# Attention with a linear branch: one step of VectorE's exponentials moved to GpSimd, with batches of four tiles

## The chip, the cores and the metric

One core of a Trainium2 chip. The metric is device time in microseconds, from runs of the whole kernel; a profile of one execution shows its span from the first to the last instruction. Engines in the text: TensorE (PE) multiplies matrices into PSUM, ScalarE (ACT) computes the exponentials, VectorE (DVE) and GpSimd (POOL) do elementwise work, SyncE (SP) issues DMAs.

## The reference

Two attention branches over the same 2048 tokens of width 512 (32 heads of 16) are mixed by a gate:

```python
g = sigmoid((x * gate_w).sum(-1, keepdims=True))
# branch A: plain softmax attention
scores = einsum("bhqd,bhkd->bhqk", q, k) * (Dh ** -0.5)
a = (softmax(scores) @ v, heads merged) @ wo
# branch B: linear attention with softmax features
phi_q = concat([softmax(q @ w_phi), softmax(-(q @ w_phi))])      # phi_k likewise
b = (phi_q @ (phi_k^T v) / (phi_q @ sum(phi_k) + 1e-6)) @ wo
return g * a + (1 - g) * b
```

Branch A's scores are 32 x 2048 x 2048 numbers, and each needs an exponential. That is the bulk of the work.

## The kernel before

**Tiles.** A score tile is 128 keys by 512 queries of one head, keys on partitions. The run goes through 512 packs (`NPACK`) of four tiles (four heads), in 32 groups of 16 packs: a group is one query chunk with four heads, and its 16 packs run over the keys. `_scores` (L977, matmuls L984) makes a tile in a PSUM bank; `_exp` (L1027, L1035) lets ScalarE take groups of three and two tiles alternately to `ET`; `_pv` (L1042, matmuls L1104) multiplies each tile by the values into the accumulator of its group; `_norm` divides and transposes on VectorE (L1157 to L1169). Five of the eight banks are the ring for ScalarE, three are shared by accumulators, projections and VectorE's tiles. The last group is cut into four blocks of 128 queries, so that its results come out one after the other.

**VectorE's tiles.** ScalarE can't do all exponentials in the time, so some tiles are done by VectorE. `SHARES` (L824) says how many in each of the 32 groups (226 in all), `SOON` adds four at the start; `_plan_vector` (L831) spreads them and cuts them into batches of `NB` = 5. `_vector_batch` (L862) makes 2^y of a batch by a cubic:

1. `v_bits` (L883), once a tile: the score from PSUM, scaled, as a uint32 fixed-point number into `vt` (two buffers, used in turn).
2. `v_frac` (L907): byte 2 of each word, the fraction, becomes an fp16 number in `vf` (one buffer).
3. `v_line` (L909), `v_sq` (L910), `v_cube` (L911): the polynomial, in `vf` and `vu` (three buffers, `NVU`).
4. `v_out` (L893): the integer part of `vt` is added to the result's bits, which then are a bf16 number.

Steps 2 to 4 work on a whole batch. The value matmuls of these tiles read `vu`.

**Branch B.** `_b_keys` and `_b_queries` project tokens and run `_b_part` (L1255), a long list of VectorE instructions (L1306 to L1359) that makes the feature softmaxes in bf16 and fp16; it uses `vt` and `vf` as scratch too. Its due times come from `K0, SK, Q0, SQ` (L1172).

**Order.** Nothing is scheduled at run time. `Plan.op` (L93) records every operation with its engine, a cost in microseconds, its buffers and a due time `prio`. `Plan.order` (L153) then walks through time with these costs: for each engine it takes the operations whose inputs are there and appends the one that can start first, the more urgent of two. The result is one fixed queue for each engine; `_waits` (L326) adds the semaphores that the dependencies need, and `emit` writes it out. An engine runs its queue strictly in order, so that an instruction that waits holds all that stand behind it. `LEAD` = 13 packs is how far ahead of its use a batch of VectorE is due. GpSimd has only constants to make, all near the start.

## Time and profile before

| what | us |
|---|---|
| median of 3 runs | 838.36 (837.57 to 838.61) |
| span of the profiled execution | 836.5 |
| VectorE's bits, L883, 226 of 512 columns | 148.3 |
| VectorE's `v_frac`, L907, 47 instructions | 67.1 |
| VectorE's `v_line` L909, `v_sq` L910, `v_cube` L911 | 37.9, 68.6, 68.5 |
| VectorE's `v_out`, L893 | 127.6 |

A line of the page's groups reads: line, engine and operation, output and input by the program's names, their shape and type, the count; then busy time and the mean length of one in ns; then the idle time of the engine in front of them and what ended it. A line of the stretches gives, for each engine, busy time and the number of instructions, then TensorE's granted clock (1.00 throughout), the DMA engines' busy share and GB/s. The time between the span and the runs' time lies outside the first and last instruction.

### The profile page before, as it was taken

The page shows a single profiled execution, that of the slowest core. Times are in us where ns is not written, and L with a number is a line of the kernel's source. Part 1 is how long each engine was busy: PE and PEld are TensorE (multiplying, and loading weights), DVE is VectorE, ACT ScalarE, POOL GpSimd, SP SyncE. Part 2 cuts the span into 40 slices and gives each one's busy share as a digit, 9 for nine tenths or more (in the row PEclk, how much of TensorE's full clock was granted, in tenths as well). Part 3 has the DMA queues.
Part 4 walks back from the last instruction along what each step waited for, and adds up shares of the span by engine and source line. Part 5 has one row for each costly group of instructions (what it writes and reads, how often), then busy time and mean ns, then how long its engine had stood idle before and what let it go on. Part 6 is the DMA issues. An engine that isn't in the chain of part 4 may idle for free.

```text
span 836.5 us, 19540 instructions
## 1 busy us (share of the span) xinstructions
PE 792.9 (95%) x8711; PEld 263.0 (31%) x8753; DVE 806.8 (96%) x1050; ACT 825.4 (99%) x733; POOL 8.0 (1%) x15
## 2 busy tenths in 40 slices
PE   9999999999999999999999999999999999999998
PEld 4323333333232222232223322222322223222234
DVE  6999999999999999999999999999998999999994
ACT  7999999999999999999999999999999999999997
POOL 3000000000000000000000000000000000000000
PEclk9999999999999999999999999999999999999999
DMA  9500000000000000210003010003100003000000
GB/s 250 157 6 8 1 7 1 2 1 8 2 7 2 7 1 8 52 22 13 1 7 59 20 33 2 4 5 70 27 15 8 1 11 79 21 8 2 2 2 27
DMA packets 49027, 20.01 MB, mean 24 GB/s; under 512 B 38704, under 2 KB 48944, under 8 KB 48944
## 3 DMA queue, kind: packets, MB, share of 16 engines
q1 hardware_dynamic: 48272, 18.58, 9.4%
q8 instruction: 68, 1.11, 0.6%
q10 hardware_dynamic: 672, 0.20, 0.1%
q14 instruction: 15, 0.12, 0.0%
HBM read 6.31 MB, written 2.10 MB: 10 GB/s over the span
## 4 chain that ended last, share of the span: by engine, by line
ACT 92%; DVE 5%; PE 2%; DMA 0%; SPq 0%; issue 0%
ACT ET L1035 92%; DVE vt L883 1%; PE ps L984 0%; DMA qT<-qraw 0%; SPq L761 0%; PE ps L633 0%; DVE vu L893 0%; PE ps L1113 0%; DVE bq L1268 0%; DVE vt L1321 0%; DVE VB L1252 0%; DVE T L1157 0%; DVE vf L907 0%; DVE vu L911 0%; DVE vf L910 0%; DVE bq L1315 0%
## 5 line engine op out<-in xcount | busy, mean ns | idle before, releaser
L1035 ACT ACTIVATE ET<-ps 128x1536 bf16<-128x1536 f32 x728 | 823.1, 1397 | 1.7 <-PE ps L984 1.5
L984 PE MATMUL ps<-qT,kT 32*128 32x512 bf16 (+2 forms) x2249 | 318.4, 364 | 31.4 <-ACT ET L1035 22.2
L1113 PE MATMUL ps<-kT,zero 128*32 128x512 bf16 (+1 forms) x3052 | 255.3, 383 | 0.0
L1104 PE MATMUL ps<-ET,V 128*32 128x512 bf16 (+2 forms) x1998 | 195.8, 364 | 1.3 <-ACT ET L1035 0.6
L984 PEld LDWEIGHTS ps<-qT,kT 32*128 32x128 bf16 x2249 | 83.5, 91 | 305.5 <-ACT ET L1035 227.1
L883 DVE TENSOR_SCALAR vt<-ps 128x512 uint32<-128x512 f32 x226 | 148.3, 681 | 3.8 <-PE ps L984 3.1
L893 DVE SCALAR_TENSOR_TENSOR vu<-vt,vu 128x2560 int16<-128x2560 uint32 (+3 forms) x47 | 127.6, 2716 | 0.7
L1113 PEld LDWEIGHTS ps<-kT,zero 128*32 128x32 bf16 x3052 | 67.9, 94 | 103.2 <-issue 78.5
L1104 PE MATMUL ps<-vu,V 128*32 128x512 bf16 (+1 forms) x250 | 85.3, 364 | 0.3 <-DVE vu L893 0.3
L1104 PEld LDWEIGHTS ps<-ET,V 128*32 128x32 bf16 x1998 | 55.0, 95 | 67.0 <-issue 36.9
L910 DVE TENSOR_TENSOR vf<-vf 128x2560 f16<-128x2560 f16 (+3 forms) x49 | 68.6, 1400 | 0.6
L911 DVE TENSOR_TENSOR vu<-vu,vf 128x2560 f16<-128x2560 f16 (+3 forms) x49 | 68.5, 1398 | 0.5
L907 DVE TENSOR_SCALAR vf<-vt 128x2560 f16<-128x2560 uint8 (+3 forms) x47 | 67.1, 1427 | 0.2
L681 PE MATMUL ps<-WB,xT 128*128 128x512 bf16 x165 | 48.8, 383 | 4.0 <-issue 1.6
L909 DVE TENSOR_SCALAR vu<-vf 128x2560 f16<-128x2560 f16 (+3 forms) x49 | 37.9, 774 | 2.0 <-PE ps L1104 1.8
L681 PE MATMUL ps<-xT,WA 128*128 128x512 bf16 (+1 forms) x124 | 35.8, 380 | 0.0
L1157 DVE STREAM_TRANSPOSE T<-ps 128x512 f32<-128x512 f32 (+1 forms) x35 | 23.2, 664 | 5.0 <-PE ps L1104 4.6
L1104 PEld LDWEIGHTS ps<-vu,V 128*32 128x32 bf16 x250 | 22.9, 96 | 11.5 <-issue 8.5
L681 PEld LDWEIGHTS ps<-WB,xT 128*128 128x128 bf16 x192 | 14.4, 97 | 27.0 <-issue 14.3
L1268 DVE TENSOR_SCALAR bq<-ps 128x512 bf16<-128x512 f32 x32 | 21.5, 679 | 0.5 <-PE ps L681 0.4
L777 PE MATMUL ps<-WA,xT 128*128 128x128 bf16 x256 | 18.9, 220 | 0.4 <-DVE vt L883 0.2
L1321 DVE TENSOR_TENSOR vt<-vt,brec 128x4096 bf16<-128x4096 bf16 (+1 forms) x10 | 18.6, 1857 | 0.0
(105 smaller groups left out, 421.8 us busy)
## 6 DMA issues: line engine op xcount, KB each, us to landing
qT<-qraw SPq DMA_DIRECT2D x120, 16.0 KB, 1.8
xn<-in_A_x_dram SPq DMA_DIRECT2D x3, 512.0 KB, 6.1
WB<-in_B_wqkv_dram SPq DMA_DIRECT2D x3, 512.0 KB, 5.0
out_dram<-WB SPq DMA_DIRECT2D x12, 128.0 KB, 1.9
WA<-in_A_wqkv_dram SPq DMA_DIRECT2D x3, 384.0 KB, 5.2
xn<-in_A_x_dram SPq DMA_DIRECT2D x2, 256.0 KB, 3.6
WoA<-in_A_wo_dram SPq DMA_DIRECT2D x1, 512.0 KB, 5.7
WoB<-in_B_wo_dram SPq DMA_DIRECT2D x1, 512.0 KB, 6.6
```

The costliest lines, as they stand in the source:

```text
L681: mm = op("PE", lambda e, c=c: e.matmul(self._bank(job)[:, 0:n], lhs(c), rhs(c), start=(c == 0), stop=(c == 3)), self.c_pe(n), reads=reads ...
L883: parts.append(op("DVE", lambda e, j=j, job=job: e.tensor_scalar(vt[:, j, :], self._bank(job), SCALE * LOG2E * 2.0 ** 24, 2.0 ** 31, op0=A ...
L893: o = op("DVE", lambda e: e.scalar_tensor_tensor(out=flat(vu).bitcast(I16), in0=flat(vt), scalar=2.0 ** -17, in1=flat(vu), op0=ALU.mult, o ...
L907: ("_frac", two, lambda e: e.tensor_scalar(vf, frac, 1 / 256, ROOT, op0=ALU.mult, op1=ALU.add), [b_vt], [b_vf]),
L909: lambda e: e.tensor_scalar(vu, vf, CUBE, SQUARE, op0=ALU.mult, op1=ALU.add), [b_vf], [b_vu]),
L910: ("_sq", two, lambda e: e.tensor_tensor(vf, vf, vf, ALU.mult), [b_vf], [b_vf]),
L911: ("_cube", two, lambda e: e.tensor_tensor(vu, vu, vf, ALU.mult), [b_vf, b_vu], [b_vu]),
L984: ins = e.matmul(out[u][:, cols], self.kT[32 * i:32 * i + 32, cp, kt * TOK:(kt + 1) * TOK], self.qT[32 * i:32 * i + 32, s, q], start=True, ...
L1035: o = plan.op("ACT", lambda e: e.activation(self.ET[:, a % NS:a % NS + n, :], self.ps[:, a % NR:a % NR + n, :], ACT.Exp, scale=SCALE), sel ...
L1104: ins = e.matmul(self._bank(ot)[32 * i:32 * i + 32, to], self.V[:, kt, g8 // 2, v0:v0 + 32], tile[:, cols], start=first and j == 0, stop=o ...
L1113: ins = e.matmul(self._bank(ot)[32 * i:32 * i + 32, lo:QCH], self.zero[:], self.kT[:, 0, lo:QCH], start=False, stop=False, tile_position=( ...
L1157: return e.transpose(to, acc if alone else acc.rearrange("p (e b d) -> p e b d", e=2, b=8))
```

## The change

The `v_frac` step of VectorE's tiles goes to GpSimd. A batch is four tiles, and GpSimd gets it in pieces of two, each of which waits only for the bits of its own two tiles, for the last readers of `vf`, and for the `v_out` of the batch before. The two small batches of `SOON` and the last two batches (`TAIL`) keep the step on VectorE. [...] `vt` has three buffers; a batch's score matmuls wait for the `v_cube` of the batch that used its buffer before, and its bits for all of that batch's readers. The shares are new (231 tiles and the four of `SOON`), as are several due times.

```diff
+        self.port = name in Plan.PORT
...
+    PORT = {"v_frac", "v_line", "v_sq", "v_cube", "v_out", "gate_z", "gate_h", "gate_b", "n_den", "n_mul", "kvbd", "b_grid", "b_rest",
+            "b_max", "b_top", "b_down", "b_square", "b_slope", "b_even", "b_odd", "b_part", "b_out", "b_sum", "b_ratio", "b_mul"}
+    GUARD, GIVE, TAKE = 0.25, 0.15, 0.12
...
+        port = {"DVE": None, "POOL": None}
...
+            pool = [(max(free["POOL"], o.dep_t, port["DVE"].end + self.GIVE if port["DVE"] else 0.0), o) for o in avail["POOL"]
+                    if o.port and o.rel <= self.now]
+            booked = min(pool, key=lambda x: x[0]) if pool else None
...
                     t = max(free[e], o.dep_t)
+                    if o.port and e == "POOL" and port["DVE"]:
+                        t = max(t, port["DVE"].end + self.GIVE)
+                    elif o.port and e == "DVE":
+                        if port["POOL"]:
+                            t = max(t, port["POOL"].end + self.TAKE)
+                        if booked and t > booked[0] - self.GUARD:
+                            t = max(t, booked[0] + booked[1].cost + self.TAKE)
...
+            if o.port and e in port:
+                other = port["DVE" if e == "POOL" else "POOL"]
+                if other is not None:
+                    o.deps.append(other)
+                port[e] = o
...
-    NB, NVU, LEAD = 5, 3, 13
-    QDUE, VPRIO, VREL, TPRIO = 28.0, -16.0, 161.0, 5
+    NB, NVU, LEAD = 4, 3, 13
+    NVT, PIECE = 3, 2
+    QDUE, VPRIO, VREL, TPRIO = 34.9956, -9.6804, 161.0, 0
...
-    OREL = 3
-    ENDS = 9
+    OREL = 0
+    ENDS = 11
+    POOL = 0.00138
+    SOONER = "_cube"
+    TAIL = 2
...
-        self.vt = nc.alloc_sbuf_tensor_at("vt", [P, 2, self.NB, QCH], I32U, offset=xn_at)
+        self.vt = nc.alloc_sbuf_tensor_at("vt", [P, self.NVT, self.NB, QCH], I32U, offset=xn_at)
...
-    SHARES = (0, 2, 2, 6, 0, 5, 4, 5, 8, 4, 9, 9, 10, 4, 15, 4,
-              2, 14, 8, 8, 12, 3, 6, 7, 14, 8, 7, 12, 6, 11, 14, 7)
+    SHARES = (0, 2, 2, 8, 0, 5, 5, 2, 11, 1, 11, 9, 14, 7, 9, 8, 3, 11, 3, 14, 5, 8, 11, 8, 14, 3, 6, 8, 10, 10, 12, 11)
...
-                   reads=self._score_bufs([u]), deps=b_vt.readers, name="vqk", prio=due + step * j, rel=due + step * j - self.VREL, kind="row",
+                   reads=self._score_bufs([u]), deps=b_vt.soon or b_vt.readers, name="vqk", prio=due + step * j, rel=due + step * j - self.VREL, kind="row",
...
-                op0=ALU.mult, op1=ALU.add), self.c_dve(512), deps=[m], name="v_bits",
+                op0=ALU.mult, op1=ALU.add), self.c_dve(512), deps=[m, *b_vt.readers], name="v_bits",
...
-            op("DVE", fn, cost, reads=reads, writes=writes, name="v" + name, prio=prio)
-        o = op("DVE", lambda e: e.scalar_tensor_tensor(
+            if name == "_frac" and not soon and number < len(self.batches) - self.TAIL:
+                o = self._frac(vt, vf, parts, b_vt, b_vf, prio)
+            else:
+                o = op("DVE", fn, cost, reads=reads, writes=writes, name="v" + name, prio=prio)
+            if name == self.SOONER:
+                b_vt.soon = [o]
+        self.last_out = o = op("DVE", lambda e: e.scalar_tensor_tensor(
...
+    def _frac(self, vt, vf, parts, b_vt, b_vf, prio):
+        free, made, at = b_vf.readers or b_vf.writers, [], 0
+        while at < len(parts):
+            n = min(self.PIECE, len(parts) - at)
+            made.append(self.plan.op(
+                "POOL", lambda e, a=at, n=n: e.tensor_scalar(
+                    vf[:, a:a + n, :], vt[:, a:a + n, :].bitcast(U8).rearrange("p n (q h) -> p n q h", h=4)[:, :, :, 2], 1 / 256, ROOT,
+                    op0=ALU.mult, op1=ALU.add), 0.2 + n * QCH * self.POOL, deps=[*parts[at:at + n], *free, self.last_out],
+                name="v_frac", prio=prio))
+            at += n
+        b_vt.readers += made
+        b_vf.writers, b_vf.readers = made, []
+        return made[-1]
...
-    K0, SK, Q0, SQ = 17.0, 8.5, 178.25, 18.0
+    K0, SK, Q0, SQ = 16.8537, 8.3684, 180.0264, 18.0212
```

More of the change, by code (lines that the diff above doesn't have):

```diff
@@ L32, in __init__ @@
         self.readers = []
+        self.soon = []
 class Job:
@@ L439, in _memory @@
         self.xn = sb("xn", [P, NT, D], BF16)
-        at[0] = max(at[0], xn_at + 2 * self.NB * QCH * 4)
-        self.vt = nc.alloc_sbuf_tensor_at("vt", [P, 2, self.NB, QCH], I32U, offset=xn_at)
+        at[0] = max(at[0], xn_at + self.NVT * self.NB * QCH * 4)
+        self.vt = nc.alloc_sbuf_tensor_at("vt", [P, self.NVT, self.NB, QCH], I32U, offset=xn_at)
         self.xT = sb("xT", [P, NT, 4, TOK], BF16)
@@ L865, in _vector_batch @@
         NB = len(units)
-        k, slot, soon = self.n_bits % 2, number % self.NVU, 2 * number < len(self.SOON)
+        k, slot, soon = self.n_bits % self.NVT, number % self.NVU, 2 * number < len(self.SOON)
         self.n_bits += not soon
@@ L884, in _vector_batch @@
                 vt[:, j, :], self._bank(job), SCALE * LOG2E * 2.0 ** 24, 2.0 ** 31,
-                op0=ALU.mult, op1=ALU.add), self.c_dve(512), deps=[m], name="v_bits",
+                op0=ALU.mult, op1=ALU.add), self.c_dve(512), deps=[m, *b_vt.readers], name="v_bits",
                 prio=due + step * j - 40, release=job))
-        b_vt.writers, b_vt.readers = parts, []
+        b_vt.writers, b_vt.readers, b_vt.soon = parts, [], []
         self.last_bits = parts
@@ L918, in _attention @@
         self.n_bits = 0
+        self.last_out = None
         self._plan_vector()
@@ L925, in _attention @@
         self.b_outt = [Buf() for _ in range(6)]
-        self.b_vt, self.b_vf, self.b_vu = [Buf() for _ in range(2)], Buf(), [Buf() for _ in range(self.NVU)]
+        self.b_vt, self.b_vf, self.b_vu = [Buf() for _ in range(self.NVT)], Buf(), [Buf() for _ in range(self.NVU)]
         for b in self.b_vt:
@@ L1274, in _b_part @@
             x.writers, x.readers = list(parts), []
-        k, n, h, ng = self.n_bits % 2, 2 * nt * QCH, nt * QCH, 16 * nt
+        k, n, h, ng = self.n_bits % self.NVT, 2 * nt * QCH, nt * QCH, 16 * nt
         self.n_bits += 1
         b_vt, b_vf = self.b_vt[k], self.b_vf
+        b_vt.soon = []
         two, four = lambda n: 0.057 + n * 0.000525, lambda n: 0.066 + n * 0.000262
```

## The prediction

> **What bounds the kernel now.** I read the busy table first, then the chain that ended last, the costliest groups, the busy time by stretches of 50 us, and last the timeline of VectorE over one batch.

> ```profile
> PE 792.9 (95%) x8711; PEld 263.0 (31%) x8753; DVE 806.8 (96%) x1050; ACT 825.4 (99%) x733; POOL 8.0 (1%) x15
> ...
> ACT 92%; DVE 5%; PE 2%; DMA 0%; SPq 0%; issue 0%
> ...
> L1035 ACT ACTIVATE ET<-ps 128x1536 bf16<-128x1536 f32 x728 | 823.1, 1397 | 1.7 <-PE ps L984 1.5
> ```

> ScalarE is the bound: 728 exponentials take 823.1 of 836.5 us, and in the whole run it waits 1.5 us for scores. A tile costs 823.1 / 1818 = 0.453 us there (2048 score tiles less the 230 that VectorE makes). TensorE's 95% holds 3052 filler matmuls (L1113) and sets nothing.

> ```profile
> 150.00:200.00 50.00, 47.28 (x497) 17.04 (x501) 49.90 (x65) 50.00 (x46) 0.00 (x0) 1.00 0.02 4
> 450.00:500.00 50.00, 47.88 (x510) 15.66 (x513) 49.86 (x56) 50.00 (x45) 0.00 (x0) 1.00 0.19 42
> 800.00:836.50 36.50, 31.58 (x673) 16.84 (x671) 25.49 (x44) 32.02 (x30) 0.00 (x0) 1.00 0.05 17
> ```

> The third busy figure is VectorE, the fourth ScalarE, the fifth GpSimd. Two engines are full side by side: VectorE is at 49.9 of 50 in mid-run, so it cannot take a tile more there; it has room only in the last 36 us, and GpSimd is empty. The stretches from 50 to 800 us lack 1.07 us of ScalarE in all (0.70, 0.31, 0.06).

> **The change, part by part.** *Tiles.* The shares give 231 + 4 = 235 tiles instead of 226 + 4, so ScalarE loses five, one pair of instructions (three tiles and two): 5 x 0.453 = 2.26 us off the path. The cumulated shares show where: up to the last group VectorE has one tile more than before (220 to 219), the last group has 11 instead of 7. So the freed time is spent in the tail, and in mid-run the same tiles are made in another way.

> *VectorE's own work.*

> ```profile
> L907 DVE TENSOR_SCALAR vf<-vt 128x2560 f16<-128x2560 uint8 x43 | 63.6, 1478 | 0.2
> L907 DVE TENSOR_SCALAR vf<-vt 128x2048 f16<-128x2048 uint8 x1 | 1.2, 1182 | 0.0
> L893 DVE SCALAR_TENSOR_TENSOR vu<-vt,vu 128x2560 int16<-128x2560 uint32 x43 | 121.2, 2818 | 0.6
> L893 DVE SCALAR_TENSOR_TENSOR vu<-vt,vu 128x2048 int16<-128x2048 uint32 x1 | 2.3, 2291 | 0.0
> ```

> Off: 43 fractions of 1.478 and the two of the first batches at 0.69: 65.0 us (the two small batches of B's start and the last two keep theirs). On: the step from five to four tiles in a batch. The other four steps take 0.813 + 1.482 + 1.479 + 2.818 = 6.59 us for five, 1.318 each; by the rows of 2048 columns 0.695 + 1.184 + 1.218 + 2.291 = 5.39 for four, 1.347 each; 0.029 x 220 = 6.3 us. Five more tiles with their bits: 5 x (0.681 + 1.347) = 10.1 us. So VectorE goes from 806.8 to about 758 us. In the stretch in which ScalarE runs (8.92 to 831.65) it is busy for 801.0 of 822.7, idle 21.7; its room becomes 21.7 + 48.6 - 2.3 = 68 us.

> *The pieces on GpSimd.* 61 batches less two at the start and two at the end leave 57: 55 of two pieces, two of one, 112 pieces of 1024 columns. No row has this operation, so bounds.

> ```profile
> L571 POOL MEMSET qT<- 128x2048 bf16 x1 | 1.8, 1804 | 0.0
> L574 POOL TENSOR_TENSOR wphi<-wphin,heads 128x512 bf16<-128x512 bf16 x1 | 1.1, 1051 | 1.5 <-DMA wphin<-in_B_w_phi_dram 1.5
> L792 POOL COPY gwb<-gw 128x16 bf16<-128x16 bf16 x1 | 0.3, 255 | 15.8 <-DMA gw<-in_gate_w_dram 15.8
> ```

> Below: a fill that reads nothing, 0.88 ns a column, 0.25 + 0.90 = 1.15 us. Above: two inputs, (1051 - 255) / 496 = 1.60 ns a column, 1.87 us. One input, a conversion and two operations is nearer to the upper row; I take 1.6. [...]

> *The two new waits.* A piece waits for the last two-port VectorE instruction ahead of it in the plan, and the next such instruction waits for the piece. Behind a waiting VectorE instruction its whole queue stands: bits, evictions of projections, transposes. For these wait TensorE (a score bank) and, through its queue, ScalarE. The handoffs: at the start GpSimd's selection ended at 1.18 + 0.29 = 1.47 and VectorE's reader began at 1.50, 0.03 us; a dependent VectorE instruction starts 0.04 us after its predecessor; GpSimd waited 0.18 us for its own fill. I take 0.2 us for both ways, between 0.07 and 0.37. Windows closed to two-port work: 112 x 1.8 = 202 us (137 to 251). VectorE can afford 68 of them idle, so 134 us, 66%, must be covered by its one-port work (50% to 73%).

> What could cover them: 235 bits and 161 evictions and transposes of 512 columns (L1268, L1252, L783, L1438, L703, L759, L1489, L1157, L1241), at a pitch of 0.60, 238 us; 56% of it must fall into windows. The timeline shows that this is roughly where it lies already:

> ```profile
> 620.95 1.49 DVE L907 TENSOR_SCALAR vf<-vt 128x2560 f16<-128x2560 uint8 x1
> 622.36 2.54 DVE L883 TENSOR_SCALAR vt<-ps 128x512 uint32<-128x512 f32 x4
> 625.44 0.69 DVE L759 CAST qraw<-ps 128x512 bf16<-128x512 f32 x1 [0.54 <-PE ps L681]
> 626.04 0.68 DVE L883 TENSOR_SCALAR vt<-ps 128x512 uint32<-128x512 f32 x1
> 626.64 0.82 DVE L909 TENSOR_SCALAR vu<-vf 128x2560 f16<-128x2560 f16 x1
> ```

> Columns are start, duration, instruction. Between a fraction and the step that reads it lie 4.3 us of one-port work; two pieces need 3.6. Four bits and two other instructions per batch fill that. I cost the windows at nothing on the path. If this cover fails, each point of it is 2.0 us of VectorE, and what is late next is the `v_out` of a batch, then the value matmuls (L1104) that read it, then the scores behind them.

> *The rest.* Three bit buffers let the bits run further ahead, a gain that only helps the cover. The shifted due times (branch B, queries, norms) have no row: at best they remove the 1.07 us of stalls, at worst they add a few like them. The tail: the last `v_out` ended at 818.5; four tiles more are 8.1 us, to 826.6 if nothing moves, while the last but one group of keys is used about three packs (1.6 us each) before ScalarE's end at 829.4; the room in front is enough if VectorE enters the tail on time. GpSimd's queue ends its old work at 26.1 us, the first fraction began at 30.1, so nothing stands in front of it; SP issues the same DMAs.

> Sum: 836.5 - 2.26 = 834.2 span. The span lies 1.9 us under the median of the runs, 838.36; so 836.1.

> **Rivals.**
> *The handoffs give the gain back.* Six or seven stalls of ScalarE of the size that the stretches show (0.31) make 2.1 us: 838.2. For it: 112 new crossings in an order fixed beforehand. Against it: before, as many crossings to TensorE cost 1.5 us in all.

> *VectorE becomes the bound* (the other side). Where tiles are densest, the second and last quarter, a batch of four has some 12 us; two-port work 5.4 + 2, windows 3.6, leaving 1 us for one-port work outside them. If cover stays at 61% where 66% is needed, 10 us are missing: 838.4 - 2.3 + 10 = 846. It decides from 66% down, or from pieces above 1.6 us: at 1.87 the windows grow by 30 us, of which a third to all comes back as time, 846 to 866. For it: VectorE at 49.9 of 50. Against: the runs of one-port work above.

> *An unguarded two-input instruction meets a piece.*

> ```profile
> L1321 DVE TENSOR_TENSOR vt<-vt,brec 128x4096 bf16<-128x4096 bf16 x6 | 13.7, 2285 | 0.0
> ```

> `b_octave` (L1321, ten instructions, 18.6 us) reads two tensors of SBUF, but its name isn't in the guarded list. If half of the ten make a piece wait or wait for one, for 1.6 us each, VectorE is 8 us late: 838.4 - 2.3 + 8 = 844. [...] Against it: ten places in 836 us, and a lead of 13 packs ahead of use.

> **Chances and range.** ScalarE still fed, 835.0 to 836.6: 0.46. Gain given back, within 0.2%: 0.16. VectorE the bound: 0.30. The unguarded instruction: 0.08. A difference of 0.2% (1.7 us) is about the least that can be told from none here. Faster 0.46, same 0.16, slower 0.38. The likeliest is 836.1. The low end, 834.8, is this with the mid-run stalls gone and 0.2 off the tail; the high end, 847, takes in VectorE as the bound at 1.6 us a piece and leaves out the long pieces.

> **What will show it.** Right: 726 exponentials, busy about 821; some 112 GpSimd instructions of about 1.6 us; VectorE busy near 758 and its waits for GpSimd under 68 us; no ScalarE waits beyond 2 us. Wrong: VectorE idle behind GpSimd for more than that, ScalarE waiting for L984 in the dense quarters, or pieces near 1.9 us.

## The result and the profile after

The changed kernel takes 839.67 us (median of 20 runs, 838.24 to 842.09), the kernel before, run beside it, 837.77 (20 runs, 837.33 to 838.65). The ratio is 1.0025, with a 95% interval of 1.0018 to 1.0031: slower by a quarter of a per cent, where 836.1 was forecast. The profiled execution has a span of 837.2 us (before 836.5) and a mean granted clock of TensorE of 0.992 (before 1.000). That is no accident of this execution: the clock was 0.988 to 0.994 in all 20, with 0.994 in the fastest (838.24) and 0.988 in the three slowest (841.59 to 842.09), while no execution of the kernel before whose clock is on record fell under 0.999.

The page of the changed kernel, in the order in which the page of before was read: the busy table, the granted clock in 40 slices, the chain that ended last, and four groups. A digit 9 of the clock's row means 90% or more of full speed.

```profile
PE 794.8 (95%) x8486; PEld 262.9 (31%) x8528; DVE 765.7 (91%) x1058; ACT 823.1 (98%) x730; POOL 123.1 (15%) x127
...
PEclk9999999999999999999989999999999999999999
...
ACT 93%; PE 6%; DVE 0%; issue 0%
...
L1079 ACT ACTIVATE ET<-ps 128x1536 bf16<-128x1536 f32 x725 | 820.9, 1375 | 4.1 <-PE ps L1028 3.8
...
L1157 PE MATMUL ps<-kT,zero 128*32 128x512 bf16 (+1 forms) x2828 | 238.4, 385 | 0.0
L936 POOL TENSOR_SCALAR vf<-vt 128x1024 f16<-128x1024 uint8 x112 | 115.1, 1045 | 663.4 <-DVE vu L922 550.3
L907 DVE TENSOR_SCALAR vt<-ps 128x512 uint32<-128x512 f32 x231 | 151.2, 683 | 32.4 <-PE ps L1028 29.0
```

Two lines of before to set beside them, the filler matmuls (now L1157) and VectorE's bits (now L907):

```profile
L1113 PE MATMUL ps<-kT,zero 128*32 128x512 bf16 (+1 forms) x3052 | 255.3, 383 | 0.0
L883 DVE TENSOR_SCALAR vt<-ps 128x512 uint32<-128x512 f32 x226 | 148.3, 681 | 3.8 <-PE ps L984 3.1
```

Most of what was planned happened. ScalarE's busy time fell by 2.2 us (825.35 to 823.12), VectorE's from 806.8 to 765.7, and the 112 pieces on GpSimd (L936) took 1045 ns each, far less than the 1.6 us that I took. But ScalarE's idle time rose from 11.2 us (836.5 - 825.35) to 14.1 (837.2 - 823.12): 2.9 more, and -2.2 + 2.9 is the 0.7 us by which the span grew. VectorE, now with room, waits 29.0 us for scores where it waited 3.1: it is no longer what is full. One digit in the clock's row says where to look, the slice around 430 us.

Busy time by stretches says the same. First the stretch from 400 to 450 us of before, then two stretches of the changed kernel (TensorE, its weight loads, VectorE, ScalarE, GpSimd, then the granted clock):

```profile
400.00:450.00 50.00, 48.02 (x511) 13.73 (x507) 48.41 (x63) 50.00 (x46) 0.00 (x0) 1.00 0.04 8
```

```profile
400.00:450.00 50.00, 45.37 (x419) 12.29 (x413) 44.73 (x57) 47.63 (x43) 6.84 (x7) 0.90 0.02 4
750.00:800.00 50.00, 46.82 (x543) 14.44 (x542) 44.95 (x50) 49.42 (x45) 10.68 (x11) 0.97 0.01 2
```

ScalarE lacks 2.37 us in the first and 0.58 in the second, and just there the clock is not full. With 1.03 us more in the first 50 us (there the clock's record begins at 6.5 us instead of 5.4, and the same 16 matmuls at 5.38 us took 1.59 us instead of 1.05; in the traces of ten kernels ScalarE is busy for 43.28 to 44.41 us of these 50) and 1.07 saved where before had its stalls, this makes the 2.9.

Inside the first stretch, again the changed kernel's busy times by windows, first the 3.41 us before the clock falls:

```profile
429.80:433.21 3.41, 0.97 (x10) 0.29 (x8) 3.41 (x3) 3.41 (x4) 0.00 (x0) 1.00 0.08 19
430.00:431.00 1.00, 0.21 (x3) 0.10 (x3) 1.00 (x2) 1.00 (x2) 0.00 (x0) 1.00 0.11 29
432.00:433.00 1.00, 0.10 (x2) 0.00 (x0) 1.00 (x1) 1.00 (x2) 0.00 (x0) 1.00 0.07 16
434.00:435.00 1.00, 0.58 (x2) 0.07 (x2) 1.00 (x1) 1.00 (x1) 0.00 (x0) 0.50 0.00 0
438.00:440.00 2.00, 2.00 (x16) 0.27 (x13) 1.38 (x3) 1.08 (x2) 0.02 (x1) 0.50 0.00 0
```

TensorE, 95% busy on the average, is busy for 0.97 of 3.41 us here (10 and 21% in the two windows of 1 us), then its clock is granted at one half. It falls at 433.2 us and comes back 10.24 us later. When the work comes back while the clock is still halved, from 438 to 440 us, TensorE is full (2.00 of 2.00) and ScalarE starves (1.08 of 2.00). The timeline of the changed kernel gives the cause (start, duration, instruction, in brackets the idle time before it and what ended it):

```profile
423.40 1.22 DVE L954 TENSOR_TENSOR vu<-vu,vf 128x2048 f16<-128x2048 f16 x1
...
430.79 0.39 PE L1028 MATMUL ps<-qT,kT 32*128 32x512 bf16 x3 [0.96 <-ACT ET L1079]
...
430.80 2.28 DVE L1366 TENSOR_TENSOR vt<-vt,brec 128x4096 bf16<-128x4096 bf16 x1
...
433.05 0.50 PE L1028 MATMUL ps<-qT,kT 32*128 32x512 bf16 x3 [0.95 <-ACT ET L1079]
433.60 2.28 DVE L922 SCALAR_TENSOR_TENSOR vu<-vt,vu 128x2048 int16<-128x2048 uint32 x1
435.94 0.13 PEld L1148 LDWEIGHTS ps<-vu,V 128*32 128x32 bf16 x2 [0.52 <-DVE vu L922]
435.97 2.05 POOL L936 TENSOR_SCALAR vf<-vt 128x1024 f16<-128x1024 uint8 x2 [16.97 <-DVE vu L922]
```

The cube of a batch (L954) ends at 424.6, but its last step, `v_out` (L922), runs only at 433.6: nine microseconds of other instructions, all but one of branch B and ending with L1366 and one more, stand between them, because their due time is 252 to 253 packs and that of `v_out` 262.4. The last value matmuls of the group (L1148) read this `vu`. Until they have run, the group's accumulator isn't finished and the next one isn't opened. The plan counts an accumulator as open for filler matmuls (L1157) only up to the value matmuls of the group's last pack, here at 429.08 us, so it has no place for them until the next one opens. So TensorE makes scores alone. Nothing here is a GpSimd wait: the next pieces come afterwards, 0.09 us after `v_out`.

The plan holds this hole from the start. By its own costs it ends at 830.72 us, 2.78 less than the plan of before (833.5); what it doesn't know is that TensorE's clock can fall, here to one half for 10.24 us. Summed over TensorE's operations of the plan with the array time that it books for each, the emptiest 3.41 us (the shortest time for which a clock stayed halved in these traces) have 42% of the array in the plan of before and 8% in this one, at 428.7. My theory from here on: **the hole costs the clock, and the clock costs the gain**. The rival is that the handoffs between VectorE and GpSimd give the gain back along the whole run.

### The profile page after: what moved, and what is told of

It reads as the page before. It is cut to its first block, busy times and chain, and to the rows that moved or that the text cites. A ratio compares the mean times of both kernels' runs of the same rounds, so it can differ in the third digit from the quotient of the medians.

```text
span 837.2 us, 19244 instructions
## 1 busy us (share of the span) xinstructions
PE 794.8 (95%) x8486; PEld 262.9 (31%) x8528; DVE 765.7 (91%) x1058; ACT 823.1 (98%) x730; POOL 123.1 (15%) x127
## 3 DMA queue, kind: packets, MB, share of 16 engines
q8 instruction: 66, 1.08, 0.5%
## 4 chain that ended last, share of the span: by engine, by line
ACT 93%; PE 6%; DVE 0%; issue 0%
ACT ET L1079 93%; PE ps L1028 2%; PE ps L1148 1%; PE ps L1157 1%; PE ps L706 1%; PE ps L658 0%; PE ps L802 0%; PE ps L740 0%; PE ps L1280 0%; PE ps L1576 0%; DVE V L808 0%; DVE bq L907 0%; PE ps L677 0%; PE ps L756 0%; DVE vf L950 0%
## 5 line engine op out<-in xcount | busy, mean ns | idle before, releaser
L1028 PE MATMUL ps<-qT,kT 32*128 32x512 bf16 (+2 forms) x2248 | 322.4, 366 | 32.0 <-ACT ET L1079 23.5
L1157 PE MATMUL ps<-kT,zero 128*32 128x512 bf16 (+1 forms) x2828 | 238.4, 385 | 0.0
L936 POOL TENSOR_SCALAR vf<-vt 128x1024 f16<-128x1024 uint8 x112 | 115.1, 1045 | 663.4 <-DVE vu L922 550.3
L1148 PE MATMUL ps<-ET,V 128*32 128x512 bf16 (+2 forms) x1980 | 197.2, 368 | 1.0 <-DVE V L808 0.3
L907 DVE TENSOR_SCALAR vt<-ps 128x512 uint32<-128x512 f32 x231 | 151.2, 683 | 32.4 <-PE ps L1028 29.0
L922 DVE SCALAR_TENSOR_TENSOR vu<-vt,vu 128x2048 int16<-128x2048 uint32 (+2 forms) x59 | 132.0, 2237 | 0.8
L1157 PEld LDWEIGHTS ps<-kT,zero 128*32 128x32 bf16 x2828 | 62.6, 95 | 98.8 <-issue 77.2
L1148 PE MATMUL ps<-vu,V 128*32 128x512 bf16 (+1 forms) x268 | 86.4, 361 | 0.0
L1148 PEld LDWEIGHTS ps<-ET,V 128*32 128x32 bf16 x1980 | 55.1, 96 | 64.6 <-issue 35.8
L953 DVE TENSOR_TENSOR vf<-vf 128x2048 f16<-128x2048 f16 (+2 forms) x61 | 71.7, 1175 | 0.9
L954 DVE TENSOR_TENSOR vu<-vu,vf 128x2048 f16<-128x2048 f16 (+2 forms) x61 | 71.7, 1175 | 0.8
L952 DVE TENSOR_SCALAR vu<-vf 128x2048 f16<-128x2048 f16 (+2 forms) x61 | 40.5, 664 | 0.0
L1148 PEld LDWEIGHTS ps<-vu,V 128*32 128x32 bf16 x268 | 23.2, 96 | 17.2 <-issue 10.3
L1366 DVE TENSOR_TENSOR vt<-vt,brec 128x4096 bf16<-128x4096 bf16 (+1 forms) x10 | 18.6, 1856 | 0.0
```

The costliest lines, as they stand in the source:

```text
L907: parts.append(op("DVE", lambda e, j=j, job=job: e.tensor_scalar(vt[:, j, :], self._bank(job), SCALE * LOG2E * 2.0 ** 24, 2.0 ** 31, op0=A ...
L922: self.last_out = o = op("DVE", lambda e: e.scalar_tensor_tensor(out=flat(vu).bitcast(I16), in0=flat(vt), scalar=2.0 ** -17, in1=flat(vu), ...
L936: "POOL", lambda e, a=at, n=n: e.tensor_scalar(vf[:, a:a + n, :], vt[:, a:a + n, :].bitcast(U8).rearrange("p n (q h) -> p n q h", h=4)[:, ...
L952: lambda e: e.tensor_scalar(vu, vf, CUBE, SQUARE, op0=ALU.mult, op1=ALU.add), [b_vf], [b_vu]),
L953: ("_sq", two, lambda e: e.tensor_tensor(vf, vf, vf, ALU.mult), [b_vf], [b_vf]),
L954: ("_cube", two, lambda e: e.tensor_tensor(vu, vu, vf, ALU.mult), [b_vf, b_vu], [b_vu]),
```

## The experiments

**The hole filled.** After the plan is made, filler blocks (four small matmuls each, adding zeros to an accumulator that is open) are put into TensorE's queue wherever the plan leaves a gap with an accumulator open: 17 blocks, one at 395 and 16 from 428 to 434 us. There they go into the accumulator that waits for its last value matmuls. Nothing else differs from the changed kernel.

```diff
+    def plug(self):
...
+            job = next((w[0] for w in lives.values() if w[1] < k <= w[2]), None)
+            if job is not None and 10 < o.start < 826:
+                at = max(x.end for x in q[max(0, k - 6):k])
+                for _ in range(int((o.start - at - 2 * self.SWITCH) / self.FILL)):
+                    x = Op("PE", self.pad(job), self.FILL, "pad", o.prio, -99, "col", 0.2, self.ALL)
...
+            p.plug()
```

> The changed kernel with 17 filler blocks (68 small matmuls that add zeros to the open accumulator) put into the gaps of TensorE's queue at about 429 to 435 us, and nothing else moved. Clock theory (the time is lost because TensorE runs nothing but scores for 6 us while a late v_out is awaited, its clock then halves for 10.2 us, and the scores come late): no half clock around 435, ScalarE's idle time between 400 and 450 us falls from 2.4 to under 0.4, span from 837.2 to about 834.4; the second half-clock stretch at 788 (3.4 us, 0.6 of ScalarE) stays, as nothing is added there. VectorE theory (VectorE is late behind GpSimd's pieces and ScalarE is starved of scores by the held queue, whatever the clock): v_out at 433.6 is no earlier, so the stall stays, span 837.

Measured: 836.15 us (11 runs, 834.95 to 838.24), ratio to before 0.9981 (0.9973 to 0.9990). The stretch of this kernel that answers to the one above:

```profile
400.00:450.00 50.00, 48.16 (x503) 13.99 (x504) 46.01 (x59) 50.00 (x45) 6.43 (x7) 1.00 0.02 4
```

84 matmuls more than in the changed kernel (503 to 419), the clock full, ScalarE without a gap, and 3.5 us come back with no instruction of VectorE or GpSimd touched. Useless matmuls made the kernel faster than before. Its clock is full in one execution of eleven only (834.95), and 0.994 to 0.998 in the others; the profiled one, at 0.998, lost it from 783.94 us for 3.41 us, at the second weak place, which this edit leaves alone.

**The order mended.** The same hole can be closed at its cause: the `v_out` of that one batch is made due 12 packs earlier.

```diff
-            self.c_dve(n), reads=[b_vt, b_vu], writes=[b_vu], name="v_out", prio=prio)
+            self.c_dve(n), reads=[b_vt, b_vu], writes=[b_vu], name="v_out", prio=prio - 12 * (250 < units[0] / 4 < 254))
```

> The changed kernel with one due time moved: the v_out of the one batch whose cube ends at 423.5 us in the plan is due 12 packs earlier, ahead of branch B's instructions. The plan still ends at 830.72 us and the same instructions are made; the lowest share of TensorE's array over 3.41 us in the plan rises from 0.08 (at 428.7) to 0.31 (at 780). Theory (TensorE's clock, lost in that one hole): no half clock near 435, ScalarE idle under 0.5 us in 400-450, span about 834.5 and time about 836.5, as with the plugged hole; the half clock near 784 may stay. Rival (the hole is a side effect, and the time goes in the GpSimd waits all along the run): unchanged, 839 to 840.

Measured: 836.41 us (11 runs, 834.94 to 837.84), ratio 0.9983 (0.9974 to 0.9992); span 833.4 in the profiled execution. Its stretch, and VectorE's timeline at the place:

```profile
400.00:450.00 50.00, 48.59 (x513) 13.93 (x508) 45.60 (x58) 50.00 (x45) 6.44 (x7) 1.00 0.02 4
```

```profile
424.14 0.69 DVE L1351 TENSOR_SCALAR vt<-bq 128x2048 bf16<-128x2048 bf16 x1
424.75 2.29 DVE L922 SCALAR_TENSOR_TENSOR vu<-vt,vu 128x2048 int16<-128x2048 uint32 x1
```

`v_out` starts at 424.75 instead of 433.60, and the 3.3 us between this kernel and the changed one are the price of one due time. Both kernels agree, and they close the hole in different ways. The three executions of this one at a full clock take 834.94 to 835.39; the others, at 0.996 to 0.998, up to 837.84. So some clock is lost in eight executions of eleven. The profiled one is at a full clock, so no trace shows where; the second weak place, near 784, is still in its plan.

**The kernel before without fillers there.** If the clock is the cause, the kernel before must lose time in the same way, with no GpSimd in it. Its fillers planned between 427.5 and 436 us are left out, 16 blocks. (The text below says 27 blocks between 422 and 438; the kernel that ran left out these 16.)

```diff
+            p.queues["PE"] = [o for o in p.queues["PE"] if o.name != "pad" or not 427.5 < o.start < 436]
```

> The kernel before, without GpSimd, with the 27 filler blocks that its plan puts between 422 and 438 us left out; every other instruction stays where it is. Clock theory: TensorE's busy share over 3.4 us falls to about 0.4 to 0.5 there, its granted clock halves for 3.4 to 10.2 us, ScalarE idles 1 to 3 us in that stretch, span 836.5 to 838 to 839. Rival (fillers only keep TensorE busy and the clock has some other cause, GpSimd's pieces for instance): clock stays 1.00, span stays 836.5, or gets shorter by a few tenths.

Measured: 839.62 us (8 runs, 838.35 to 843.01), ratio 1.0023 (1.0012 to 1.0034), as slow as the changed kernel. The profiled execution is the slowest of the eight (843.01, clock 0.988; the others have 0.991 to 0.996). Three windows of it, and what ScalarE waited for in it (in all, times, longest):

```profile
428.40:431.81 3.41, 2.07 (x19) 0.49 (x15) 3.41 (x4) 3.41 (x4) 0.00 (x0) 1.00 0.00 0
430.00:432.00 2.00, 1.11 (x9) 0.29 (x9) 2.00 (x4) 2.00 (x4) 0.00 (x0) 0.95 0.00 0
436.00:438.00 2.00, 1.98 (x17) 0.36 (x15) 2.00 (x4) 2.00 (x3) 0.00 (x0) 0.50 0.10 25
```

```profile
ACT ET L1036 <- PE ps L985: 5.4, 6, 1.8
```

The fillers compute nothing that is used, and without 16 blocks of them the clock was halved for 20.48 us in this execution, from 431.81, and ScalarE waited 5.4 us; a median execution lost less of it. This settles that a lack of fillers alone makes this kernel slower by as much as the change did.

**The waits taken away.** The order in the queues stays that of the changed kernel, but the waits that keep the pieces and VectorE's instructions in `PORT` (the prediction's two-port ones) apart are left out.

```diff
-                other = port["DVE" if e == "POOL" else "POOL"]
-                if other is not None:
-                    o.deps.append(other)
```

> The changed kernel in the same order on every engine, but without the waits that keep a GpSimd piece and a two-port VectorE instruction apart; only the waits for data are left. If the two exclude each other in hardware for a whole instruction: pieces that meet a two-port instruction show up to 2.3 us instead of 1.045, or the VectorE instruction is longer by up to 1.0; few meet, as a piece already waits for the last v_out by its data. VectorE's busy time 766 to 785 us; the hole at 430 us is untouched, so span 836.5 to 838. If they don't exclude each other: pieces stay at 1.045, VectorE's rows stay, span the same 837.

Measured: 839.23 us (838.70 to 841.64), ratio 1.0018 (1.0009 to 1.0027): the loss stays, so these waits aren't where it goes. (A piece still waits for the bits it reads and for the last `v_out`.) The order alone keeps the two apart nearly always; once they met. VectorE's timeline of this kernel, then GpSimd's:

```profile
655.65 1.04 DVE L1348 TENSOR_SCALAR vt<-bq 128x2048 bf16<-128x2048 bf16 x1
```

```profile
655.10 2.49 POOL L933 TENSOR_SCALAR vf<-vt 128x1024 f16<-128x1024 uint8 x2 [8.58 <-DVE vu L919]
```

The VectorE instruction, 0.69 us elsewhere, took 1.04 beside a piece, and the pair of pieces 2.49 instead of 2.05.

**The fraction back on VectorE.** Batches of four, 235 tiles and three bit buffers stay; every batch keeps its fraction on VectorE, and the plan orders the queues anew.

```diff
-    TAIL = 2
+    TAIL = 1000
```

> The changed kernel with the fraction step of all batches back on VectorE; shares, batches of four, three bit buffers and due times as in the change, so the plan orders the queues anew. If the offload carries the five more tiles: VectorE has to take 65 us more, is full again as before (above 98% from 100 to 800 us), comes late, and ScalarE waits 8 to 12 us in all; span 843 to 848. If the offload is worth nothing: within 1 us of the changed kernel, 837.

Measured: 846.87 us (846.46 to 847.50), ratio 1.0103 (1.0088 to 1.0119). Busy table and ScalarE's wait:

```profile
PE 800.8 (95%) x8726; PEld 266.1 (31%) x8772; DVE 819.2 (97%) x1115; ACT 823.2 (97%) x730; POOL 8.1 (1%) x15
```

```profile
ACT ET L1079 <- PE ps L1148: 9.9, 4, 3.0
```

Here VectorE is the bound, and ScalarE waits 9.9 us behind value matmuls that wait for `vu`. The pieces on GpSimd are worth 7.2 us in this plan (846.87 to 839.67): the offload itself works. It is not its gain over the best kernel without it, as the other constants were chosen for the offload.

**The guard taken out of the plan.** With an empty `PORT` the plan is made anew, as if pieces and the instructions named there didn't disturb each other.

```diff
-    PORT = {"v_frac", "v_line", ...
+    PORT = set()
```

> The changed kernel with an empty list of guarded names, so that the plan is made anew and neither orders nor waits for the ports: by the plan about 30 instructions of branch B (b_sum, b_out, b_part, b_grid) lie beside a GpSimd piece. If a two-port or two-input instruction and a piece exclude each other: where the two meet, the later one is longer by up to the rest of the earlier one (a piece up to 1.045 + 1.2 us, an instruction of 2048 columns up to 1.2 + 1.0), 10 to 25 us over all; as the plan books 1.6 us for a piece of 1.05, most of that is paid already, so the span stays within 1 us of what the plan's order gives. If they share the ports: all pieces 1.05, all instructions as in the changed kernel. On the time: the plan keeps TensorE's filled share above 0.34 over 3.4 us (0.08 in the changed kernel, 0.42 before), so the clock theory expects at most one or two half-clock stretches of 3.4 us instead of 10.2 at 435; the new order has 2.5 us of stalls of its own at 197 and 594 us: span 836 to 839.

Measured: 844.18 us (843.38 to 844.98), ratio 1.0076 (1.0059 to 1.0093). That was above the 836 to 839 expected. Two lines around a meeting, GpSimd's timeline, then VectorE's:

```profile
178.30 3.93 POOL L935 TENSOR_SCALAR vf<-vt 128x1024 f16<-128x1024 uint8 x2 [29.98 <-DVE bq L1382]
```

```profile
179.88 1.45 DVE L1386 TENSOR_TENSOR vt<-bq 128x2048 f16<-128x2048 bf16 x1
```

Two pieces took 3.93 us instead of 2.05, and the two-input VectorE instruction that ran into them 1.45 instead of 1.21. The first piece, 1.96 us, began 0.16 us after another two-input instruction, which took its usual 1.21 us and ran to 179.35: 1.05 us of that instruction were left, and the piece was longer than its own 1.05 by 0.91. So it was held up for most of what was left. Over the run 14 pieces were longer, by 9.9 us in all. The plan of this kernel ends at 834.83, 4.1 us after that of the changed kernel, with constants that were chosen for the guarded order; and its span lies 7.5 us above its plan, where most lie 2 to 3 above theirs (below). These 5 us more are what is left for the collisions; that they are all due to them isn't shown by a run of its own. The guard, which I had costed as a burden, keeps them away.

**The plan made again with the measured piece.** Two kernels have the cost of a piece at its measured 1.045 us and new shares, due times and margins of the guard, 243 tiles each; more of the last batches (`TAIL`) keep the step on VectorE, so 98 and 108 pieces are left on GpSimd. One of them was picked so that the emptiest 3.41 us of its plan have at least 41% of TensorE's array, the other by the planned end alone (its emptiest has 33%). In both, a diff of constants; of the second:

```diff
-    GUARD, GIVE, TAKE = 0.25, 0.15, 0.12
+    GUARD, GIVE, TAKE = 0.2, 0.12, 0.12
...
-    NB, NVU, LEAD = 4, 3, 13
+    NB, NVU, LEAD = 4, 3, 17
-    QDUE, VPRIO, VREL, TPRIO = 34.9956, -9.6804, 161.0, 0
+    QDUE, VPRIO, VREL, TPRIO = 37.8215, -20.9042, 161.0, 15.9875
-    POOL = 0.00138
+    POOL = 0.000825
-    TAIL = 2
+    TAIL = 6
...
+    SHARES = (0, 2, 1, 8, 0, 5, 4, 3, 12, 2, 12, 8, 11, 8, 13, 9, 7, 11, 1, 14, 6, 10, 10, 7, 14, 5, 5, 3, 14, 10, 13, 11)
-    K0, SK, Q0, SQ = 16.8537, 8.3684, 180.0264, 18.0212
+    K0, SK, Q0, SQ = 17.5986, 8.456, 185.4364, 18.3851
```

> The offload with a plan made anew: a piece is booked at the 1.045 us that the trace of the changed kernel shows instead of 1.613, and shares and due times were chosen so that TensorE's planned share of full-array work over any 3.4 us stays at 0.41 or above (0.42 before, 0.08 in the changed kernel); 243 tiles instead of 235. The plan ends 2.2 us before that of the changed kernel and 5.0 before that of the kernel before; measured spans lay 2.4 to 3.0 us behind their plans where the clock held. Clock theory: clock 1.00 throughout, span 831 to 832, time 833, ratio 0.994. VectorE theory (handoffs and VectorE's lateness set the time): eight tiles more make it worse, ScalarE waits for scores by more than 3 us, span above 834.

> The same with shares and due times chosen for the planned end alone, without the floor under TensorE's share: 243 tiles too, the plan ends 0.5 us earlier than with the floor, but TensorE's share falls to 0.33 at about 485 and at 603 us. Clock theory: half-clock stretches of 3.4 us or more at one or both of these places in most executions, 0.5 to 2 us of ScalarE lost there, so not faster than the run with the floor, and its times spread wider. If a share of 0.33 is still enough: clock 1.00, span 830.5 to 831.5, faster than with the floor by about 0.5.

Measured: with the floor 832.70 us (832.11 to 833.12), ratio 0.9937 (0.9925 to 0.9950); without it 832.11 (832.00 to 832.55), ratio 0.9932 (0.9919 to 0.9946). The clock was full in all five executions of both. So both beat the kernel before by 5 to 6 us. What the second expectation said of a plan with 33% of the array in its emptiest window, half-clock stretches in most executions, did not come; the other case that it named did. The busy table of the second:

```profile
PE 800.8 (96%) x8624; PEld 266.1 (32%) x8624; DVE 783.4 (94%) x1078; ACT 819.2 (99%) x727; POOL 119.1 (14%) x123
```

**The kernel before, with its due times chosen anew.** Is the gain of these two only a better choice of constants? The kernel before, without GpSimd, got the same kind of search over the same constants.

```diff
-    NB, NVU, LEAD = 5, 3, 13
-    QDUE, VPRIO, VREL, TPRIO = 28.0, -16.0, 161.0, 5
+    NB, NVU, LEAD = 5, 3, 11
+    QDUE, VPRIO, VREL, TPRIO = 28.107, -23.1662, 161.0, 2.5405
...
-    K0, SK, Q0, SQ = 17.0, 8.5, 178.25, 18.0
+    K0, SK, Q0, SQ = 17.3805, 8.543, 177.6723, 17.7954
```

> The kernel before, without GpSimd, with its shares (230 tiles and four), LEAD, QDUE, VPRIO, TPRIO and branch B's due times chosen anew by planned end, as for the kernel with 243 tiles: the plan ends at 832.1 us instead of 833.5, and the lowest share of TensorE's array is 0.33. If the offload is what carries the tiles, new due times alone give no more than the plan says, 1.4 us: span about 834.8, time about 836.4. If the gain of the kernels with 243 and 239 tiles was the retuning alone, this one comes to 833 or below.

(Both offloaded kernels have 243 tiles; 239 is the sum of their shares.) Measured: 837.26 us (11 runs, 835.81 to 839.76), ratio 0.9990 (0.9981 to 0.9999). At a full clock it takes 835.8 to 836.1; in seven of eleven executions it loses some of it (0.994 to 0.998). Retuning alone gave 0.7 us in the median and 2 at a full clock; the search was a limited one, so a better plan without GpSimd isn't excluded.

**All plans side by side.** The plan's own end, its emptiest 3.41 us of TensorE's array, and the spans measured (median, or of the executions at a full clock where the clock varied):

| kernel | plan's end | emptiest | span | span - plan |
|---|---|---|---|---|
| before | 833.5 | 0.42 | 836.0 | 2.5 |
| changed | 830.7 | 0.08 | 837.2 | 6.5 |
| changed, `v_out` mended, full clock | 830.7 | 0.31 | 833.1 to 833.6 | 2.6 |
| before, due times anew, full clock | 832.1 | 0.33 | 834.0 to 834.3 | 2.1 |
| before without the 16 blocks | 833.5 | 0.18 | 837.8 | 4.3 |
| fraction on VectorE | 842.5 | 0.31 | 845.0 | 2.5 |
| no guard | 834.8 | 0.34 | 842.4 | 7.5 |
| 243 tiles, with the floor | 828.5 | 0.41 | 830.9 | 2.4 |
| 243 tiles, without | 828.0 | 0.33 | 830.3 | 2.3 |

Six of nine lie 2.1 to 2.6 above their plan (in the middle, where a range stands). The three that don't are the two that lost the clock in every execution, with 0.08 and 0.18, and the one whose pieces collide. Kernels with an emptiest share of 0.31 to 0.34 sometimes kept the clock and sometimes not; with 0.41 and above they lost next to nothing (0.999 at the least, in the runs of before). The emptiest place isn't always where it goes: in the profiles of the kernel with the fraction on VectorE and of the one before with due times anew the clock fell at 746.87 and 620.77, behind places to which their plans give 0.36 (at 742 and 616 us), and not behind their emptier ones.

## Why the prediction was wrong

**The step that failed** is the sentence "TensorE's 95% holds 3052 filler matmuls (L1113) and sets nothing", and with it the bound on the shifted due times, "at worst they add a few like them", a few stalls of 0.3 us. The fillers set the clock: without 16 blocks of them the kernel before ran at 0.988 to 0.996, with them at 0.999 or 1.000. The new plan opened a hole in them (2828 are left), the clock was halved, and ScalarE lost 2.37 us at one place and 0.58 at another, more than the 2.2 us that the change won. The cost of a halved clock was in no term and in no rival. With the hole closed by one due time the kernel takes 836.41, with fillers put into it 836.15; 836.1 was forecast. I had named the order of what is late (`v_out`, then the value matmuls, then the scores), but tied it to a failing cover of the windows. It was late because something else was due earlier.

**The gain** was sized rightly: 2.26 us forecast, 2.2 measured, and the sum of 834.2 for the span was 833.4 and 834.1 in the two mended kernels' profiles. That their medians (836.41, 836.15) meet the 836.1 so closely is in part luck: both still lose some clock in most executions, and at a full clock they take 834.9 to 835.4. There the 1.07 us of mid-run stalls are gone too (in the profile with `v_out` mended ScalarE is never idle from 50 to 800 us), which the forecast had only as the best case. And it started from 838.36, the median of three runs; from the 837.77 of twenty the same gain would give 835.5.

**The pieces** were mis-sized: 1.6 us taken, 1.15 as the lower bound, 1.045 measured (1.044 to 1.047 over all). The fill that gave the lower bound, with a start of 0.25 us and 0.90 for its columns, was no lower bound for this step. The handoff from VectorE to GpSimd was 0.09 us, one way, where I allowed 0.07 to 0.37 for both. So the closed windows are some 130 us (112 x (1.05 + 0.1)), not 202, and 88 of the pieces' 117 us (112 x 1.045), by the trace's records, lay beside VectorE's work: three quarters, where two thirds of the longer windows were asked for.

**VectorE's busy time** came out at 765.7 where 758 was worked out. The durations summed fell by 46.9 us (879.7 to 832.8), close to the 48.6 forecast. But neighbouring instructions overlap a little and the busy time counts that once: 879.7 - 806.8 = 72.9 us of overlap before, 832.8 - 765.7 = 67.1 after. I had left these 5.8 us out. That a queue which waits more often overlaps less is my reading; no run tests it.

**The rivals.** "VectorE becomes the bound" did not happen: the waits that the profile puts down to GpSimd's pieces are 1.6 us, once, where 68 were allowed. The kernel with the fraction back on VectorE shows what it looks like when VectorE does bind: 846.87, with ScalarE waiting for value matmuls. "The handoffs give the gain back" named a time near the measured one for another reason: without the waits 839.23 remain. The unguarded `b_octave` (L1366 in the listing of after) never met a piece; that two-input instructions and pieces hold each other up, which no trace of before showed, is shown by the kernel without the guard (3.93 us for two pieces instead of 2.05, 1.45 for the instruction instead of 1.21). "Two-port" in the prediction is a name for the instructions in `PORT`: that they use two ports is shown by no run. What the runs show is that such an instruction and a piece take longer where they meet, while VectorE's bits, which often lay beside pieces, took 683 ns (before 681).

**What stays open.** The time outside the span is 1.8 us for all kernels but the changed one and the one without waits, where it is 2.04 in the median and up to 3.03; no run takes that apart. What lowers the clock is known by its effect and not by an exact threshold. TensorE's busy time doesn't give one: 3.41 us with 2.30 busy (changed, at 784.78), 2.41 (hole filled, 780.53) and 2.97 (before with due times anew, 617.36) were followed by a halved clock, and 2.48 (`v_out` mended, 780.54) and 2.46 (before, 814.25) were not. The second weak place, near 784, wasn't mended alone, and which of the changed constants (due times, shares, the 1.6 us booked for a piece) put `v_out` behind branch B wasn't tried.

## What to carry to other kernels

Look at the granted clock before calling an engine's filler work free: where matmuls are there to keep the array loaded, a reordering on another engine can take them away, and the price falls on whoever waits for TensorE next (2.37 us of ScalarE at one place here). When a plan's own end and the measured span part, find the place where they part, look at what is scarce in that window, and mend that alone: one due time was worth 3.3 us here. An offload changes the plan as much as the work, so judge it with a plan made for it, using the measured cost of the moved step.

## What the runs showed of the hardware

**GpSimd is quick at this step.** 1024 columns of one byte in four, converted to fp16 with a multiply and an add, took 1045 ns; VectorE's 2048 columns took 1182 ns before, so GpSimd works at a little over half VectorE's speed here (2.05 to 2.09 us for the same 2048).
